# Ways out of PSUM in the first unit, and a filter block by sums, in a two-layer H3 and GEGLU kernel

## The chip, the cores and the metric

The kernel runs on one core of one Trainium2 chip, as one launch. The metric is the device time of one execution in microseconds (us); the median of a few runs is given, and one more execution was taken with the hardware profiler. The granted TensorE clock was 1.00 throughout.

## The reference, cut to what matters

Two layers over 2048 tokens of width D = 576, with the same weights twice:

```python
def A(q, k, v, shift_k, ssm_k, ssm_D):          # H3 mixer
    kv = causal_shift_conv(k, shift_k) * v       # 4 taps
    y = irfft(rfft(pad(kv)) * rfft(pad(ssm_k)))  # causal convolution, length 2048, per channel
    return q * (y + kv * ssm_D)

def B(x, w_gate, w_up, w_down):                  # F = 4608
    return (gelu(x @ w_gate) * (x @ w_up)) @ w_down

x = A_q
for layer in range(2):
    x = x + A(layernorm(x), A_k, A_v, A_shift_k, A_ssm_k, A_ssm_D)
    x = x + B(layernorm(x), B_w_gate, B_w_up, B_w_down)
```

The inputs are bfloat16. `k`, `v` and the filter `ssm_k` are the same in both layers, so the mixer's `y` is made once per token and used twice.

## The kernel before, in words

**Units.** The tokens lie in four chunks of 512. A unit is one chunk of one layer's GEGLU; there are eight. They run in five passes, unit 0 alone, three passes of two units, and the last unit alone. Each unit is cut into three phases of 12 f-tiles of 128. A phase first makes gate and up for its 12 f-tiles and then adds the down product of these 12 to the residual. A gate/up tile is 18 matmuls (L1585: nine blocks of 64 contraction rows, gate and up side by side in the two row halves of TensorE) into one PSUM tile `gu`, of two banks, gate in one and up in the other. ScalarE takes gelu of the gate bank into `ga` (L1589), VectorE multiplies `ga` by the up bank into `hT` (L1590), which releases the PSUM tile. The pool `pr` has three such tiles. The down product (L1605) takes the four blocks j of 128 tokens one after another, each 24 matmuls over the 12 f-tiles, two halves of D to each; f-tile `fi` is read by matmuls 2 fi and 2 fi + 1 of a block. In unit 0, phase 0 comes in two token halves (`half_gu`, L1510 to L1514), 6 + 6 tiles of two f-tiles each, since the second half's input isn't there yet.

**Convolution.** It is done in blocks of 512 tokens: the transform of the filter block (H), that of kv (kc), their products summed over pairs of blocks (z), and an inverse (L389) whose result ScalarE copies out (`keep_y`, L395). Every transform is a few matmuls of 288 columns with constant matrices `W`. `quarter` makes a transform by four sums: four visits to TensorE of two matmuls each (L289), each copied out by ScalarE into an `eo` tile (L292), then sums and differences on VectorE (`apart` L252, `odd` L257, `even` L265). H of filter block 1 was made another way: row 2 in the startup (L214) and rows 0, 1 and 3 by full transforms and sums (`h1_rest`: L214, L223) during unit 0.

**What sets the order.** The program order of every engine is decided when the kernel is built. A planner keeps an estimated time per engine (`t.pe`, `t.act`, `t.dve`, with costs such as `C_HT` and `C_GU`). After every gate/up tile and every down step it calls `fill`, which places queued VectorE work of the convolution and of the norms up to a limit, then ScalarE's, then visits of the convolution to TensorE, and the loads and DMA transposes that have come due (`weights`, `run_loads`, `spreads`). Each engine then works strictly in this order. Weight loads (`wgu`, `wd`), the transposes of the filter (`turn`, L429) and those that make the next unit's `xnT` (`spread`, L1290) are issued by SyncE; `k`, `v`, spills and reloads of H and kc by GpSimd.

**Around the change.** During unit 0 the convolution of block 1 is finished: H1 and kc 1, z 1, then the inverse in four visits (132.0, 135.1, 138.3, 141.4 us), each into the single PSUM tile `cps`. Its y gives the second chunk's input, which is normalised and transposed into `xnT` of unit 1 (SyncE, 143.6 to 156.3 us). Unit 1 begins at 158.35 us.

Of the kernel before, what the change touches and what calls it, by code (L numbers as in the profile page):

```python
# [39 lines left out]
C_TT, C_ST, C_HT, C_GELU, C_EVA, C_EVD = 0.76, 0.82, 0.69, 0.6, 0.66, 0.76  # L40
# [44 lines left out]
class Conv:  # L85
# [9 lines left out]
    def __init__(self, spare, tc, ctx, pace, A_k, A_v, A_shift_k, A_ssm_k, A_ssm_D, ident, psp, cpsp, ypool):  # L95
# [31 lines left out]
        self.h1_at = {2: 0.0}  # L127
        self.z_at, self.then = {}, []
        self.load_at, self.tight, self.turning = -9.0, lambda: False, lambda: False
        self.nps = 0  # L130
        self.ps_free = self.spare_free = self.last = 0.0
        self.window = -1.0
        self.pr_free = [0.0] * N_SM
        self.neo, self.eo_free = 0, [0.0] * N_EO
# [108 lines left out]
    def quarter(self, src, out, h, ready, seen, done):  # L243
# [3 lines left out]
        A, slots = {}, {}  # L247
# [7 lines left out]
        def even():  # L255
            for kt, op in ((0, add), (2, sub)):
                tt(out=out()[kt][:, :, cols], in0=A[2][:], in1=A[3][:], op=op)  # L257
            when = t.on_dve(2 * C_R4)
            self.eo_free[slots[2]] = self.eo_free[slots[3]] = when
            done(0, h, when + LAG)  # L260

        def odd():
            for kt, ops in ((1, (add, sub)), (3, (sub, add))):
                for s in range(2):
                    tt(out=out()[kt][:, s, cols], in0=A[0][:, s, :], in1=A[1][:, 1 - s, :], op=ops[s])  # L265
            when = t.on_dve(4 * C_BF)
            self.eo_free[slots[0]] = self.eo_free[slots[1]] = when
            done(1, h, when + LAG)
# [3 lines left out]
        def when():  # L272
            at = [g[1] for g in going]
            if todo:
                at.append(self.slot_at())
            return max(ready(), self.eo_slot(), min(at))

        def one(n):
            def run():
# [11 lines left out]
                A[i], slots[i] = self.eo_tile("eo")  # L291
# [32 lines left out]
    def eo_tile(self, name):  # L324
        slot = self.neo % N_EO
        self.neo += 1
        self.eo_free[slot] = NEVER
        return self.eop.tile([P, 2, HW], F32, tag="eo", name=name), slot

# [112 lines left out]
    def filt(self, b):  # L442
# [23 lines left out]
        for h in range(2):  # L466
            self.Pq.extend(self.quarter(lambda: own["t"], out, h, lambda: max(own.get("at", NEVER), self.z_at[b - 1]()), seen, done))
            self.Pq.extend(self.then)
            self.then = []

    def step(self, m, kv=None, loaded=False):
# [60 lines left out]
        for kt, a in pairs:  # L532
            self.L.append((lambda kt=kt, a=a: max(self.hr_free[self.nhr % N_HR] if (m, a) != (1, 0) else 0.0,
# [155 lines left out]
        for h in range(2):  # L689
            if h == 1 and m == 1:  # L690
                self.Pq.extend(self.rest[:4])
            self.Pq.extend(self.quarter(lambda: self.vt_[m], out4, h, get(("kv", h)), seen4, done4))
        if m == 1:
            self.Pq.extend(self.rest[4:])
# [14 lines left out]
        zt = lambda mt: get(("z", mt)) if quad else zs  # L709
        out = [(lambda g=zt(mt): max(g(), self.y_used.get(m - 2, NEVER) if m > 1 else 0.0), cost, inv(mt), m) for mt in range(RT)]  # L710
        if m == 2:
            self.then = out
        else:
# [62 lines left out]
    def h1_rest(self):  # L776
        nc, t = self.nc, self.t

        own = {}

        def even(s):
            def run():
                own.update(self.pair_tile(), free=NEVER, eo=self.spare())
                self.fwd_sum(own["ps"], self.hT1, 1, s, 0)
                nc.scalar.copy(out=self.halves(own["eo"][:]), in_=own["ps"][:, :, 0:HW])
                self.last = own["at"] = t.on_act(C_EVA, t.pe + 0.49 + LAG) + LAG
            return run

        def odd(s):
            def run():  # L790
                it = dict(own)
                self.fwd_sum(it["ps"], self.hT1, 1, s, 1)
                nc.scalar.copy(out=self.halves(self.H1[:, 1, s, :]), in_=it["ps"][:, :, 0:HW])
                self.last = done = t.on_act(C_EVA, t.pe + 0.49 + LAG) + LAG

                def fin():
                    self.differ(self.H1[:, 3, s, :], it["eo"], it["ps"])
                    when = own["free"] = t.on_dve(C_R4, t.pe) + LAG
                    self.pair_done(it, max(done, when))
                    if s == 1:  # L800
                        for k in (1, 3):
                            self.h1_at[k] = when
                            self.spill(self.Hd[1][k], self.H1[:, k, :, :], when)
                self.U.append((t.pe + 0.49 + LAG, C_R4, fin))
            return run

        def full(kt, s):
            def run():
                self.fwd_full(self.hT1, kt, s, self.H1[:, kt, :, :])
                self.ps_free = t.on_act(C_EVA, t.pe + 0.98 + LAG)  # L810
                if s == 1:
                    self.h1_at[kt] = self.ps_free + LAG
                    self.spill(self.Hd[1][kt], self.H1[:, kt, :, :], self.ps_free + LAG)
            return run
        tasks = [((lambda: max(own.get("free", 0.0), self.slot_at()), 0.49, even(s), None, "pair"),
                  (lambda: own["at"], 0.49, odd(s), None, "pair")) for s in range(2)]
        first = [(lambda: 0.0, 0.98, full(0, s)) for s in range(2)]
        self.rest = [first[0], tasks[0][0], first[1], tasks[0][1], *tasks[1]]

    def begin(self, head, tables):  # L820
# [4 lines left out]
        with ExitStack() as es:  # L825
# [9 lines left out]
            full = tmp.tile([P, 256], BF16, name="full")  # L835
# [8 lines left out]
            wx = [tmp.tile([P, RT, DW], BF16, name=f"wx{i}") for i in range(2)]  # L844

# [5 lines left out]
            nc.vector.memset(full[:], 1.0)  # L851
# [19 lines left out]
            def busy(n):  # L871
                for _ in range(n):
                    nc.tensor.matmul(idle[:, 0, 0:256], lhsT=full[:, 0:P], rhs=full[:], start=True, stop=True)  # L873
# [188 lines left out]
            h_part(1, 2, 0, None, small())  # L1062
            rest = h_part(1, 2, 1, None, new(), True)
# [4 lines left out]
            rest()  # L1068
            self.spill(self.Hd[1][2], self.H1[:, 2, :, :])
# [20 lines left out]
def ssm_geglu_kernel(ctx, tc, A_q, A_k, A_v, A_shift_k, A_ssm_k, A_ssm_D, B_x, B_w_gate, B_w_up,  # L1090
# [83 lines left out]
    def sum_task(c, j, v):  # L1174
        def run():
            v["s"] = small.tile([P, 1], F32, tag="s", name="s")
            junk = work.tile([P, D], BF16, tag="ga", name="junk")
# [11 lines left out]
    def square_task(get_x, v):  # L1189
        def run():  # L1190
            v["ss"] = small.tile([P, 1], F32, tag="ss", name="ss")
            junk = work.tile([P, D], BF16, tag="ga", name="junk")
# [57 lines left out]
    def prep(ui, j):  # L1250
# [3 lines left out]
        def norm(ready):  # L1254
# [4 lines left out]
            xn_made.append((ui, j, xn, t.on_act(C_NA, max(ready, t.pe - 1.0)) + 0.3))  # L1259

        def norm_v(j):
            def run():
# [5 lines left out]
                xn_made.append((ui, j, xn, t.dve + C_NV + 0.3))  # L1268
# [33 lines left out]
    def run_vq(limit):  # L1302
# [11 lines left out]
        if r > max(t.pe + 0.2, t.dve):  # L1314
# [39 lines left out]

    def fill(limit, tensor, conv_first):
        weights()
        conv.run_loads()
        spreads()
        while True:
# [10 lines left out]
        if tensor and (hurry() or t.pe > conv.last + (CHAINED if chained() else 0.0)):  # L1370
            for _ in range(3):
                if not conv.run_p():
                    break

    with tc.manual_schedule():
# [97 lines left out]
        def first_half(hT):  # L1473
# [7 lines left out]
            for n in range(FP // 2):  # L1481
                half_gu(hT, n, 0)
                t.pe += C_GU
                if n == 0:
# [7 lines left out]
                elif n < 4:  # L1492
                    j = 2 * n - 3
                    turn0(j)
                    copy0(j, nc.scalar.copy)
                if n == 2:
                    t.dve = t.act = t.pe + 1.6
                elif n > 2:
                    t.on_dve(C_HT, t.on_act(C_GELU, t.pe + 0.15) + 0.15)
# [3 lines left out]
        def half_gu(hT, n, half):  # L1503
            pair = psp.tile([P, 2, 512], F32, tag="pr", name="gu")
            xnT, tok = xnT_of[0], slice(half * 2 * P, (half + 1) * 2 * P)
            for e in range(2):
                w, gi = wgu[(2 * n + e) // FG], (2 * n + e) % FG
                for k in range(NKC):
                    for s, r0 in ((0, 0), (1, HK)):
                        nc.tensor.matmul(pair[:, s, e * 256:(e + 1) * 256], lhsT=w[r0:r0 + HK, k, gi * P:(gi + 1) * P],  # L1510
                                         rhs=xnT[r0:r0 + HK, blk_of[k], tok], start=(k == 0), stop=(k == NKC - 1))
            ga = work.tile([P, CH], F32, tag="ga", name="ga")
# [7 lines left out]
        for m in range(2, NCH):  # L1520
# [6 lines left out]
        at_start = {(0, 2): [("es", 1), ("prep", 1)], (1, 0): [("x", 2)], (2, 1): [("es", 2)],  # L1527
# [10 lines left out]
        conv.tight, conv.turning = chained, turns_near  # L1538
        visits = []
# [3 lines left out]
        for wb, ph, ui, first, final in visits:  # L1543
# [25 lines left out]
            if wb == 0:  # L1569
                first_half(hT)  # L1570
                for n in range(FP // 2):
                    half_gu(hT, n, 1)
                    t.pe = max(t.pe, free.popleft()) + C_GU
                    free.append(t.on_dve(C_HT, t.on_act(C_GELU, t.pe + 0.15) + 0.15) + 0.1)
# [3 lines left out]
            for fi in range(FP if wb else 0):  # L1578
# [9 lines left out]
                ga = work.tile([P, CH], F32, tag="ga", name="ga")  # L1588
                nc.scalar.activation(out=ga[:], in_=pair[:, 0, :], func=ACT.Gelu_apprx_tanh)  # L1589
                nc.vector.tensor_tensor(out=hT[:, fi, :], in0=ga[:], in1=pair[:, 1, :], op=ALU.mult)  # L1590
                free.append(t.on_dve(C_HT, t.on_act(C_GELU, t.pe + 0.15) + 0.15) + 0.1)
                if gi == FG - 1 and final:
                    when_due(t.pe + (FP - FG) * C_GU + 12.0, load_wgu, n + 3)
                fill(t.pe + C_GU + (HURRY if hurry() else LEAD), now(), conv.left > 0)
            conv.window = t.pe + RT * FP * C_DN - SPARE if wb < NWB - 1 else -1.0
# [100 lines left out]
```

## Time and profile before

| | us |
|---|---|
| Median of 3 runs | 915.8 (915.63 to 916.01) |
| Profiled execution | 916.32 |
| Its span | 914.3 |
| TensorE busy | 907.3 |
| VectorE, ScalarE, GpSimd busy | 577.3, 321.8, 160.6 |
| Start of gate/up in unit 0 | 39.47 |
| Down phases of unit 0 begin | 66.25, 106.43, 146.48 |

Lines of the timeline have: start, busy time, engine, line, operation, output<-input, shape, number of instructions in the row, and in brackets the idle time before it with what ended it. A row may hold several instructions, and their starts overlap with the end of the one ahead, so a step is read from start to start. Lines of the windows have the busy time and the number of instructions of each engine, then granted clock, DMA share and GB/s. Lines of DMA issues end with the median time from issue to landing. PE is TensorE, DVE VectorE, ACT ScalarE, POOL GpSimd, SP SyncE.

### The profile page before, as it was taken

How to read it: one execution, taken by the hardware profiler on the slowest of the kernel's cores; microseconds unless marked ns; L12 is line 12 of the kernel's file. 1: busy time of each engine (PE TensorE's matmuls, PEld its weight loads, DVE VectorE, ACT ScalarE, POOL GpSimd, SP SyncE). 2: the span in 40 equal slices, each digit the busy share in tenths (PEclk: the TensorE clock that was granted, in tenths of full speed). 3: DMA queues.
4: the chain of work that ended last, by engine and by line, in shares of the span. 5: the costliest groups of instructions: out<-in, count | busy, mean ns of one | idle time of the engine just before them, and what ended most of it. 6: DMA issues, size and time to landing. Idle time of an engine off the chain costs nothing.

```text
span 914.3 us, 19277 instructions
## 1 busy us (share of the span) xinstructions
PE 907.3 (99%) x8198; PEld 528.2 (58%) x8198; DVE 577.3 (63%) x982; ACT 321.8 (35%) x602; POOL 160.6 (18%) x334
## 2 busy tenths in 40 slices
PE   8999999999999999999999999999999999999998
PEld 6786556465565564654655655646646546556555
DVE  7988977479889885685698897443333335333332
ACT  6843255533214235452224124551121224321211
POOL 3512124320115032240013202220000003100000
PEclk9999999999999999999999999999999999999999
DMA  9999986939528619675734902950720821967620
GB/s 254 324 258 256 196 181 129 274 126 197 170 79 193 190 14 155 170 182 129 179 95 103 252 24 60 179 127 17 140 79 1 156 78 27 173 166 176 137 64 27
DMA packets 128954, 131.14 MB, mean 143 GB/s; under 512 B 43618, under 2 KB 120675, under 8 KB 128868
## 3 DMA queue, kind: packets, MB, share of 16 engines
q1 hardware_dynamic: 119232, 93.47, 48.3%
q0 software_dynamic: 9632, 36.43, 12.1%
q8 instruction: 64, 1.05, 0.5%
q14 instruction: 22, 0.18, 0.1%
q10 hardware_dynamic: 4, 0.01, 0.0%
HBM read 108.35 MB, written 11.80 MB: 131 GB/s over the span
## 4 chain that ended last, share of the span: by engine, by line
PE 98%; DVE 1%; ACT 1%; issue 0%; DVEq 0%; ACTq 0%
PE gu L1585 59%; PE dn L1605 31%; PE gu L1510 3%; PE ps L214 1%; PE cps L389 1%; PE cps L289 1%; DVE wx L936 0%; PE ps L389 0%; PE ps L289 0%; PE cps L214 0%; PE cps L873 0%; DVE wx L939 0%; ACT junk L1193 0%; PE xps L1403 0%; DVE v L930 0%; PE ps L950 0%
## 5 line engine op out<-in xcount | busy, mean ns | idle before, releaser
L1585 PE MATMUL gu<-xnT,wgu 64*128 64x512 bf16 x4968 | 540.8, 376 | 0.0
L1585 PEld LDWEIGHTS <-wgu 64*128 64x128 bf16 x4968 | 239.5, 94 | 294.4 <-issue 5.9
L1589 ACT ACTIVATE ga<-gu 128x512 f32<-128x512 f32 x276 | 164.6, 597 | 481.0 <-PE gu L1585 472.4
L1590 DVE TENSOR_TENSOR hT<-ga,gu 128x512 bf16<-128x512 f32 x276 | 189.5, 686 | 213.3 <-ACT ga L1589 211.1
L1605 PE MATMUL dn<-wd,hT 128*128 128x288 bf16 x2304 | 292.1, 286 | 0.0
L1605 PEld LDWEIGHTS <-hT 128*128 128x128 bf16 x2304 | 223.6, 98 | 65.4 <-issue 9.3
L1641 DVE TENSOR_TENSOR x_c<-x_c,dn 128x576 f32<-128x576 f32 x64 | 48.1, 752 | 57.3 <-PE dn L1605 57.3
L1185 POOL TENSOR_SCALAR nm<-s 128x1 f32<-128x1 f32 x60 | 22.0, 366 | 268.2 <-DVE x_c L1636 203.2
L1193 ACT ACTIVATE junk<-x_c,nm 128x576 bf16<-128x576 f32 x48 | 36.9, 769 | 30.1 <-POOL nm L1185 28.5
L1201 POOL TENSOR_TENSOR rstd<-ve,neghalf_t 128x1 f32<-128x1 f32 x62 | 41.8, 675 | 5.2
L529 POOL DMA_DIRECT2D hr<-Hd x32 | 17.5, 548 | 116.4 <-DVE prod L348 110.9
L1200 POOL TENSOR_SCALAR ve<-ss 128x1 f32<-128x1 f32 x62 | 25.2, 406 | 54.9 <-ACT junk L1193 54.7
L1257 ACT ACTIVATE xn<-x_c,nb,rstd 128x576 bf16<-128x576 f32 (+1 forms) x50 | 29.8, 644 | 6.9 <-POOL nb L1205 6.7
L1627 DVE TENSOR_TENSOR ob<-x_c,dn 128x576 bf16<-128x576 f32 x15 | 11.3, 754 | 23.1 <-PE dn L1605 20.8
L1510 PE MATMUL gu<-xnT,wgu 64*128 64x256 bf16 x432 | 24.6, 269 | 0.0
L292 ACT COPY eo<-cps 128x576 f32<-128x576 f32 x26 | 16.6, 637 | 19.3 <-PE cps L289 16.0
L349 DVE TENSOR_TENSOR prod<-prod 128x576 bf16<-128x576 bf16 x48 | 22.0, 458 | 1.7
L1510 PEld LDWEIGHTS <-wgu 64*128 64x128 bf16 x432 | 20.8, 94 | 3.4 <-issue 0.7
L404 POOL DMA_DIRECT2D out_dram<-ob x12 | 6.7, 558 | 81.7 <-DVE ob L1627 61.2
L252 DVE SCALAR_TENSOR_TENSOR eo<-eo 128x576 f32<-128x576 f32 x20 | 14.9, 753 | 6.6 <-ACT eo L292 6.6
L1235 DVE SCALAR_TENSOR_TENSOR x_c<-g_t,rstd,x_c 128x576 f32<-128x576 f32 x16 | 13.0, 814 | 9.3 <-POOL rstd L1201 9.3
L587 DVE TENSOR_TENSOR zs<-sum,prod 128x576 f32<-128x576 bf16 x24 | 18.1, 754 | 0.3
(168 smaller groups left out, 557.8 us busy)
## 6 DMA issues: line engine op xcount, KB each, us to landing
wgu<-in_B_w_gate_dram SPq DMA_DIRECT2D x45, 576.0 KB, 5.8
wd<-in_B_w_down_dram SPq DMA_DIRECT2D x30, 864.0 KB, 6.9
wgu<-in_B_w_up_dram SPq DMA_DIRECT2D x45, 512.0 KB, 8.0
hr<-Hd POOLq DMA_DIRECT2D x32, 288.0 KB, 4.7
kr<-Kd POOLq DMA_DIRECT2D x24, 288.0 KB, 4.7
Kd<-kc POOLq DMA_DIRECT2D x12, 288.0 KB, 5.1
k<-in_A_k_dram POOLq DMA_DIRECT2D x3, 1008.0 KB, 11.5
wgu<-in_B_w_up_dram SPq DMA_DIRECT2D x45, 64.0 KB, 7.6
```

What stands on the lines that cost most here:

```text
L349: nc.vector.tensor_tensor(out=dst, in0=pr[:, 0, :], in1=pr[:, 1, :], op=ALU.subtract if part == 0 else ALU.add)
L1185: nc.gpsimd.tensor_scalar(out=v["nm"][:], in0=v["s"][:], scalar1=-1.0 / D, scalar2=None, op0=ALU.mult)
L1193: nc.scalar.activation(out=junk[:], in_=get_x(), func=ACT.Square, bias=v["nm"][:, 0:1], accum_out=v["ss"][:])
L1200: nc.gpsimd.tensor_scalar(out=ve[:], in0=v["ss"][:], scalar1=1.0 / D, scalar2=EPS, op0=ALU.mult, op1=ALU.add)
L1201: nc.gpsimd.tensor_tensor(out=v["rstd"][:], in0=ve[:], in1=neghalf_t[:, 0:1], op=ALU.pow)
L1257: nc.scalar.activation(out=xn[:, lo:hi], in_=x_c[c][:, j, 0:hi - lo], func=ACT.Identity, scale=v["rstd"][:, 0:1], bias=v["nb"][:, 0:1])
L1510: nc.tensor.matmul(pair[:, s, e * 256:(e + 1) * 256], lhsT=w[r0:r0 + HK, k, gi * P:(gi + 1) * P], rhs=xnT[r0:r0 + HK, blk_of[k], tok], sta ...
L1585: nc.tensor.matmul(pair[:, s, :], lhsT=w[r0:r0 + HK, k, gi * P:(gi + 1) * P], rhs=xnT[r0:r0 + HK, b, :], start=(k == 0), stop=(k == NKC - 1))
L1589: nc.scalar.activation(out=ga[:], in_=pair[:, 0, :], func=ACT.Gelu_apprx_tanh)
L1590: nc.vector.tensor_tensor(out=hT[:, fi, :], in0=ga[:], in1=pair[:, 1, :], op=ALU.mult)
L1605: nc.tensor.matmul(part[h][:, h, 0:HW], lhsT=hT[:, fi, at * P:(at + 1) * P], rhs=wd[2 * wb + fi // WT][:, fi % WT, h * HW:(h + 1) * HW], s ...
L1641: nc.vector.tensor_tensor(out=xh, in0=xh, in1=acc[:, :, 0:HW], op=ALU.add)
```

## The change

- **H of filter block 1** is made wholly by `quarter`, in eight visits of two matmuls. As its `eo` tiles are needed elsewhere, the sums lie in tiles lent from the reload buffers `hr` and one spare tile. The row made in the startup goes there too. Visits lie in the first half tiles and the first down phase.
- **Unit 0's gates and ups** leave PSUM by ScalarE alone in 13 pairs of tiles (4 in phase 0, 6 in the second phase, 3 in the third): gelu to bfloat16 `ga2`, and a copy of up, rounded to bfloat16, into `hT`. VectorE then multiplies two tiles in one instruction from SBUF into `hT`. `fill` places that multiply at its start once the planner takes the pair for ready; a pair that is left when the loop over f-tiles ends is placed behind the last `fill`.
- **Block 1's inverse** comes in two visits of two, the second of each in a tile borrowed from `pr`.
- **The filter's turns.** `turn(2)` comes inside unit 0's first down phase, `turn(3)` in the second; block 2's first quarters move from the second unit's first down phase to the down phase ahead of unit 1. The load of `k` for block 2 waits until the transposes into unit 1's `xnT` have been issued in the plan (`clear`). Planner constants for the norms of unit 1 move, `junk` takes another buffer during unit 0, and `full` shares the memory of `wx`.

```diff
@@ quarter
-                A[i], slots[i] = self.eo_tile("eo")
+                A[i], free[i] = self.lent_tile() if lent else self.sum_tile()
@@ the steps of block m
-            self.L.append((lambda: max(self.kv_at.get(m - 1, NEVER), self.td_at.get(self.NB - 1, NEVER)), lk))
+            self.L.append((lambda: max(self.kv_at.get(m - 1, NEVER), self.td_at.get(self.NB - 1, NEVER), self.clear()), lk))
...
+            if (m, n) == (1, 2):
+                self.turn(2)
...
+        def inv_two(mts):
+            def run():
+                ...
+                two = [(mt, pool.tile([P, 2, 512], F32, tag=tag, name="ps"))
+                       for mt, pool, tag in zip(mts, (self.cpsp, self.psp), ("cps", "pr"))]
+                for n, (mt, ps) in enumerate(two):
+                    self.inverse(m, mt, self.terms(mt, z), ps)
+                    self.keep_y(m, mt, ps)
+                    ...
+        elif m == 1:
+            self.Pq.extend((zs, 2 * cost, inv_two(mts), m) for mts in ((0, 1), (2, 3)))
@@ h1_rest: the full transforms and sums go
+        out = lambda: {kt: self.H1[:, kt, :, :] for kt in range(RT)}
+        self.rest = [q for h in range(2) for q in self.quarter(lambda: self.hT1, out, h, lambda: 0.0, lambda h: None, done, True)]
@@ startup
-            h_part(1, 2, 0, None, small())
-            rest = h_part(1, 2, 1, None, new(), True)
...
-            rest()
-            self.spill(self.Hd[1][2], self.H1[:, 2, :, :])
@@ fill
+        while made and made[0][0] <= max(t.pe + 0.2, t.dve):
+            run_made()
@@ gates and ups
+        def hidden(dst, pair, e, count):
+            if e == 0:
+                while len(made) > 1:
+                    run_made()
+                two["ga"] = work.tile([P, 2, CH], BF16, tag="ga", name="ga2")
+            ga = two["ga"]
+            nc.scalar.activation(out=ga[:, e, :], in_=pair[:, 0, :], func=ACT.Gelu_apprx_tanh)
+            nc.scalar.copy(out=dst[:, e * count:(e + 1) * count, :], in_=pair[:, 1, :].rearrange("p (f q) -> p f q", f=count))
+            when = t.on_act(2 * C_GELU, t.pe + 0.15)
+            if e == 1:
+                made.append((when + 0.15, lambda: nc.vector.tensor_tensor(
+                    out=dst, in0=ga[:].rearrange("p e (f q) -> p (e f) q", f=count), in1=dst, op=ALU.mult)))
+            return when + 0.1
@@ the loop over f-tiles
+                if ui == 0 and (fi % 2 and rounded or fi % 2 == 0 and conv.left > 0):
+                    rounded = True
+                    free.append(hidden(hT[:, fi - fi % 2:fi - fi % 2 + 2, :], pair, fi % 2, 1))
+                else:
+                    rounded = False
                     ga = work.tile([P, CH], F32, tag="ga", name="ga")
                     ...
                 fill(t.pe + C_GU + (HURRY if hurry() else LEAD), now(), conv.left > 0)
+            conv.borrowed = None
+            while made:
+                run_made()
```

More of the change, by code (lines that the diff above doesn't have):

```diff
@@ L241, in fwd_eo, with quarter @@
         return eo, slot
-    def quarter(self, src, out, h, ready, seen, done):
+    def quarter(self, src, out, h, ready, seen, done, lent=False):
         nc, t = self.nc, self.t
         cols = slice(h * HW, (h + 1) * HW)
-        A, slots = {}, {}
+        A, free = {}, {}
         add, sub = ALU.add, ALU.subtract
@@ L328, in eo_tile, with sum_tile, lent_tile, free @@
         return self.eop.tile([P, 2, HW], F32, tag="eo", name=name), slot
+    def sum_tile(self):
+        tile, slot = self.eo_tile("eo")
+        return tile, lambda when: self.eo_free.__setitem__(slot, when)
+    def lent_tile(self):
+        at, self.nlent = self.nlent % 4, self.nlent + 1
+        if at == 3:
+            self.lent_free, tile = NEVER, self.spare()
+            def free(when):
+                self.lent_free = when
+        else:
+            slot, tile = self.nhr % N_HR, self.hrp.tile([P, 2, HW], F32, tag="hr", name="eo")
+            self.hr_free[slot] = NEVER
+            self.nhr += 1
+            def free(when):
+                self.hr_free[slot] = when
+        return (self.halves(tile[:]) if at == 3 else tile), free
+    def lent_slot(self):
+        return (self.lent_free if self.nlent % 4 == 3 else self.hr_free[self.nhr % N_HR]) - 0.7
     def eo_slot(self):
@@ L466, in filt @@
         for h in range(2):
-            self.Pq.extend(self.quarter(lambda: own["t"], out, h, lambda: max(own.get("at", NEVER), self.z_at[b - 1]()), seen, done))
+            self.Pq.extend(self.quarter(lambda: own["t"], out, h, lambda: max(own.get("at", NEVER), self.z_at[b - 1](), self.clear()), seen, done))
             self.Pq.extend(self.then)
@@ L531, in load @@
             return run
-        for kt, a in pairs:
-            self.L.append((lambda kt=kt, a=a: max(self.hr_free[self.nhr % N_HR] if (m, a) != (1, 0) else 0.0,
+        for n, (kt, a) in enumerate(pairs):
+            if (m, n) == (1, 2):
+                self.turn(2)
+            self.L.append((lambda kt=kt, a=a: max(self.hr_free[self.nhr % N_HR] if (m, a) != (1, 0) else 0.0, NEVER if (m, a) == (1, 1) and self.nlent < 8 else 0.0,
                                            self.kr_free[self.nkr % 3] if a < m else 0.0,
@@ L776, in h1_rest @@
     def h1_rest(self):
[L777 to L816, printed above, removed]
@@ L817, in h1_rest, with done @@
-        first = [(lambda: 0.0, 0.98, full(0, s)) for s in range(2)]
-        self.rest = [first[0], tasks[0][0], first[1], tasks[0][1], *tasks[1]]
+        def done(kt, h, when):
+            if h == 1:
+                for k in (kt, kt + 2):
+                    self.h1_at[k] = when
+                    self.spill(self.Hd[1][k], self.H1[:, k, :, :], when)
+        out = lambda: {kt: self.H1[:, kt, :, :] for kt in range(RT)}
+        self.rest = [q for h in range(2) for q in self.quarter(lambda: self.hT1, out, h, lambda: 0.0, lambda h: None, done, True)]
@@ L872, in busy @@
                 for _ in range(n):
-                    nc.tensor.matmul(idle[:, 0, 0:256], lhsT=full[:, 0:P], rhs=full[:], start=True, stop=True)
+                    nc.tensor.matmul(idle[:, 0, 0:256], lhsT=full[:, 0:P], rhs=full, start=True, stop=True)
             busy(8)
@@ L1176, in run @@
             v["s"] = small.tile([P, 1], F32, tag="s", name="s")
-            junk = work.tile([P, D], BF16, tag="ga", name="junk")
+            junk = junk_tile()
             nc.scalar.activation(out=junk[:], in_=x_b[c][:, j, :], func=ACT.Copy, accum_out=v["s"][:])
@@ L1191, in run @@
             v["ss"] = small.tile([P, 1], F32, tag="ss", name="ss")
-            junk = work.tile([P, D], BF16, tag="ga", name="junk")
+            junk = junk_tile()
             nc.scalar.activation(out=junk[:], in_=get_x(), func=ACT.Square, bias=v["nm"][:, 0:1],
@@ L1353, in chained, with run_made, junk_tile @@
         return bool(aq or nq) or need is not None and not (need[0] == "y2" and need[1:3] not in conv.y_at)
+    made = deque()
+    def run_made():
+        ready, run = made.popleft()
+        run()
+        t.on_dve(C_H2, ready)
+    def junk_tile():
+        return work.tile([P, D], BF16, tag="ob" if unit0 else "ga", name="junk")
+    unit0 = [0]
     def fill(limit, tensor, conv_first):
@@ L1373, in fill @@
                     break
+        if unit0 and conv.borrowed:
+            while run_vq(limit, t.pe + C_GU):
+                pass
     with tc.manual_schedule():
@@ L1511, in half_gu @@
                                          rhs=xnT[r0:r0 + HK, blk_of[k], tok], start=(k == 0), stop=(k == NKC - 1))
+            if not old:
+                return lambda: hidden(hT[:, 4 * (n // 2):4 * (n // 2) + 4, tok], pair, n % 2, 2)
             ga = work.tile([P, CH], F32, tag="ga", name="ga")
@@ L1587, in ssm_geglu_kernel @@
                 t.pe = max(t.pe, free.popleft()) + C_GU
[L1588 to L1591, printed above, removed]
+                if ui == 0 and (fi % 2 and rounded or fi % 2 == 0 and conv.left > 0):
+                    rounded = True
+                    free.append(hidden(hT[:, fi - fi % 2:fi - fi % 2 + 2, :], pair, fi % 2, 1))
+                else:
+                    rounded = False
+                    ga = work.tile([P, CH], F32, tag="ga", name="ga")
+                    nc.scalar.activation(out=ga[:], in_=pair[:, 0, :], func=ACT.Gelu_apprx_tanh)
+                    nc.vector.tensor_tensor(out=hT[:, fi, :], in0=ga[:], in1=pair[:, 1, :], op=ALU.mult)
+                    free.append(t.on_dve(C_HT, t.on_act(C_GELU, t.pe + 0.15) + 0.15) + 0.1)
+                if conv.borrowed:
+                    free.popleft()
+                    free.append(conv.borrowed)
+                    conv.borrowed = None
                 if gi == FG - 1 and final:
@@ L1594, in ssm_geglu_kernel @@
                 fill(t.pe + C_GU + (HURRY if hurry() else LEAD), now(), conv.left > 0)
+            conv.borrowed = None
+            while made:
+                run_made()
+            if ui == 0 and end:
+                unit0.clear()
             conv.window = t.pe + RT * FP * C_DN - SPARE if wb < NWB - 1 else -1.0
```

64 lines of the change are left out of this document (40 added, 24 removed).

## The prediction

> **What bounds the kernel now.** I read the page's busy times and chain first, then the windows, then single stretches of the timeline. The page:
>
> ```profile
> PE 907.3 (99%) x8198; PEld 528.2 (58%) x8198; DVE 577.3 (63%) x982; ACT 321.8 (35%) x602; POOL 160.6 (18%) x334
> ...
> PE 98%; DVE 1%; ACT 1%; issue 0%; DVEq 0%; ACTq 0%
> ...
> L1590 DVE TENSOR_TENSOR hT<-ga,gu 128x512 bf16<-128x512 f32 x276 | 189.5, 686 | 213.3 <-ACT ga L1589 211.1
> ```
>
> PE is the bound: of its 7.0 us without work 3.8 lie in the first 40 us and 3.2 behind the last matmul. In between it never stops, as the windows show for the stretch that holds nearly all of the change:
>
> ```profile
> 40.00:147.00 107.00, 107.00 (x1153) 68.13 (x1150) 91.88 (x159) 44.95 (x87) 23.01 (x44) 1.00 0.94 218
> ```
>
> (PE busy 107.00 of 107.00; DVE 91.88; ACT 44.95; granted clock 1.00; DMA share 0.94.) So after 40 us only two things count: PE work that is added or removed, and any place where PE must now wait. A shorter DVE or ACT queue is worth nothing by itself. The span is 914.3, the execution 916.32, 0.5 above the median 915.8; I sum differences and set them on the median.
>
> **Matmuls removed: -1.96.** H1 of filter block 1 took 16 matmuls of L214 in the startup and 16 of L214 plus 16 of L223 between 67.7 and 79.7; four sums need 8 visits of two, 16 in all. In the profile eight L214 matmuls hold PE for .98 (67.72 to 68.70), .1225 each. Behind 40 us that is 32 before and 16 after: 16 x .1225 = 1.96. The startup's 16 are in the next step.
>
> **Startup: -0.3.** The other 16 matmuls (1.96) and two ACT copies of H (.62 each) also go. Yet DVE works without a gap from 25 to 37.2 and its list there is unchanged. What is freed is a PE wait for ACT ahead of the inverse of Y3:
>
> ```profile
> 38.39 1.14 PE L389 MATMUL ps<-yb,W 128*128 128x288 bf16 x8 [0.67 <-ACT xnT L1410]
> ```
>
> So gate and up start some .7 earlier, at about 38.7 instead of 39.47. The fourth half tile, however, needs the PSUM that DVE's second hT multiply releases, and DVE is late there:
>
> ```profile
> 45.38 0.69 DVE L1514 TENSOR_TENSOR hT<-ga,gu 128x512 bf16<-128x512 f32 x1
> 46.12 1.14 PE L1510 MATMUL gu<-xnT,wgu 64*128 64x256 bf16 x17
> ```
>
> 45.38 + .69 = 46.07, and PE goes on at 46.12. That time stays; PE waits there instead. All that is kept is one quarter visit (two matmuls, .25 to .35) which the change puts ahead of this point: -0.3, with bounds 0 and -0.75 (had DVE been early).
>
> **Two visits instead of four: -0.42.** Block 1's inverse interrupts gate and up:
>
> ```profile
> 132.00 1.15 PE L389 MATMUL cps<-yb,W 128*128 128x288 bf16 x8
> 133.08 2.12 PE L1585 MATMUL gu<-xnT,wgu 64*128 64x512 bf16 x18
> 135.13 1.15 PE L389 MATMUL cps<-yb,W 128*128 128x288 bf16 x8
> ```
>
> One round is 135.13 - 132.00 = 3.13. Eight matmuls in a row cost .98, a gate/up tile of 18 elsewhere 1.95 (23.4 for 12): .20 is lost at each change of shape and back. The whole phase, 118.36 to 146.55, gives .21. Two fewer: -.42. The first visit comes no earlier, as z is complete on DVE at 130.33 and the visit at 132.00 was within 1.7 of that.
>
> **A late quarter: +0.2.** One visit of a later filter now falls inside a gate/up phase; a quarter there took .35 instead of .25 and the tile behind it .08 longer, +.19. The other quarters only change their place inside down phases, where two 288-wide shapes follow each other at .1225.
>
> **Pairs in unit 0: nothing for the arithmetic.** Thirteen pairs: ACT does gelu and a copy per tile, DVE one bf16 product of 1024 per pair. No row has that product. The 1152-wide one takes .75 and the 576-wide .46, so by the line between them .69 (bounds .46 and 1.22, the 1024-wide product from PSUM at 13.81). DVE drops 26 x .69 = 17.9 and gains 13 x .69 = 9.0; the four sums add about 9 (L252 .75, L265 .37, L257 .7). ACT gains 26 copies of about .57 (a 576-wide copy from PSUM, L292, takes .64), 15 us in a stretch where it is busy 45 of 107. PSUM comes free about 1.2 behind the last matmul of a tile (gelu starts .1 after it, .50 to the copy, .6), while three buffers leave 3.9: cover 2.7, enough for any single ACT row (.96 the longest). With two such rows queued ahead it would still hold.
>
> The Trainium skill ("VectorE: DVE Perf Modes", Rules for kernel authors) says of products on matmul output to take the slow rate, or to copy out of PSUM first if many operations follow; here one follows. The rows side with the rule on engine time (9 us less DVE for 15 us more ACT), and by it the pairs would best be left out: the sum would lose the stall of the next paragraph and be 913.5.
>
> **A new wait: +1.5.** In the phase from 83 to 118 (second third of unit 0) the last pair is multiplied only after the filter work that the planner places behind the last tile. Before, the last multiply stood early enough:
>
> ```profile
> 103.89 1.42 DVE L363 TENSOR_TENSOR yb<-zs 128x576 bf16<-128x576 f32 x2
> 105.22 0.69 DVE L1590 TENSOR_TENSOR hT<-ga,gu 128x512 bf16<-128x512 f32 x1
> 105.83 0.75 DVE L346 TENSOR_TENSOR prod<-kr,H 128x1152 bf16<-128x1152 bf16 x1
> 106.61 0.46 DVE L349 TENSOR_TENSOR sum<-prod 128x576 bf16<-128x576 bf16 x1
> 106.99 0.75 DVE L348 TENSOR_TENSOR prod<-kr,H 128x1152 bf16<-128x1152 bf16 x1
> 107.78 0.46 DVE L349 TENSOR_TENSOR sum<-prod 128x576 bf16<-128x576 bf16 x1
> 108.15 0.68 DVE L1590 TENSOR_TENSOR hT<-ga,gu 128x512 bf16<-128x512 f32 x1
> ```
>
> The down phase starts at 106.43 and reaches f-tile 11 with matmul 22, at 106.43 + 22 x .1225 = 109.13; hT was there at 108.83. Now count from the start T of that down phase in the changed kernel. Tile 9 ends two tiles earlier, T - 3.90; gelu, copy: its pair can be multiplied at T - 2.66. The changed order then puts on DVE: that product .60, two yb sums .78, a product .79 and its half .49, zs .79, two yb 1.33, a product .78 and half .38 (spacings of L370, L346, L349, L587, L363), 5.9 in all; the last pair starts at T + 3.25 and is done at T + 3.9. PE needs f-tile 10 with matmul 20, at T + 2.45. The weight load (.1) included, PE waits 1.5. Bounds: 0 if the filter work shortens by that much, 2.2 if the 1024-wide product costs its upper bound. The other two phases end with no such work ahead.
>
> **k against the last transposes: +0.2.** The load of k for block 2 (1008 KB, POOL) moves into the end of unit 0, between the transposes that make unit 1's xnT. Two windows of before, first without and then with such a load:
>
> ```profile
> xnT<-xn SPq DMA_TRANSPOSE x2, 2.5
> ```
>
> ```profile
> k<-in_A_k_dram POOLq DMA_DIRECT2D x1, 1008.0 KB, 6.1
> xnT<-xn SPq DMA_TRANSPOSE x2, 4.6
> ```
>
> Before, the last transpose was issued at 155.01, landed at 157.5 and unit 1 began at 158.35, 3.34 after the issue. Two quarter visits now stretch the down phase behind it by .98, so 4.3. Alone the transpose needs 2.5, beside k 4.6: late by 0.3, taken as +0.2; bounds 0 and 2.1 (6.4, as between 172 and 174).
>
> **Sum.** -1.96 - 0.30 - 0.42 + 0.19 + 1.5 + 0.2 = -0.8; 915.8 - 0.8 = **915.0**. The turns of the filter move earlier on SP, ahead of weight loads; those land over 15 us before their use, which covers the 7 to 8.4 of a turn. With that cover gone, PE would wait for a weight load.
>
> **Rivals.** A: the wait of 1.5 does not arise, because DVE reaches the last pair in time. For: DVE has been relieved of 9 us, and PE need only be as slow as the chain. Against: the chain begins at a copy, not at a backlog, so relief elsewhere does not shorten it. Then -2.3 to -2.5: 913.4. B: the change's pairs are no faster than the products from PSUM (1.22 for two): DVE gets 16 instead of 9 us, the last pair is .55 later, 915.6; same verdict as the forecast. C, slower: k's megabyte holds unit 1's transposes. Next to two loads of wd and one of x_b they took far longer:
>
> ```profile
> xnT<-xn SPq DMA_TRANSPOSE x1, 10.9
> ```
>
> At 8.5 to 10.9 instead of 4.6 the last lands 4.2 to 6.6 after PE wants it: 919 to 921. It turns slower than before once the transpose takes over 5.3, and measurably so from about 7.1. For: wgu is issued 1.3 behind the last transpose too, and DMA is at a share near 1. Against: k alone gave 4.6. The Trainium skill ("DMA: Bandwidth & Descriptors", Issuing engines are not separate DMA queues) has all queues share the same 16 engines, so POOL's queue would be no shelter; the 2.5 and 4.6 agree.
>
> **How the numbers follow.** About 0.2% (1.8 us: below 914.0, above 917.6) is what a measurement of this kernel can tell from no change. The forecast with B and the smaller half of C's prices: 0.48. A: 0.36; it takes in stalls below .5 and a startup that keeps more of its .75. C and whatever other wait costs over 2.6: 0.16. Range 912.9 (A with the whole startup) to 917.8; the likeliest case alone holds 914.2 to 916.2.
>
> **What would show it.** PE rows: 8166 matmuls. A PE idle of about 1.5 some 2.5 us into the down phase near 106, released by DVE at the pair's multiply; half of the rivals falls with that one line. The inverse as two rows of x16 some 1.95 + .2 apart from gate/up. The fourth half tile still near 46.1, with a PE idle ahead of it. At unit 1's first matmul an idle of 0 to .5, released by DMA; over 3 would mean C. Wrong would be: a PE idle elsewhere, above all for ACT's release of PSUM or at filter block 2's earlier visits.

## The result, and the profile after

The changed kernel takes 920.78 us (median of 5, 919.29 to 922.01) against 916.01 for the kernel before (5 runs): a ratio of 1.0051, 95% interval 1.0036 to 1.0066. It is slower, by 4.8 us; the forecast was 915.0 in a range of 912.9 to 917.8. The profiled execution took 919.29 with a span of 917.5, so 3.2 above the span of before. The other 1.5 up to the median is not in this execution; the first experiment finds it.

From the page after, the lines that answer to those of before:

```profile
PE 902.6 (98%) x8166; PEld 526.5 (57%) x8166; DVE 577.1 (63%) x983; ACT 334.3 (36%) x628; POOL 160.1 (17%) x334
...
PE 92%; DVE 3%; DMA 2%; ACT 1%; SPq 1%; POOL 1%; issue 0%; DVEq 0%; POOLq 0%; ACTq 0%
```

PE has 32 matmuls less and works 4.7 us less, yet the span is longer: its time without work went from 7.0 to 14.9. The chain that ended last says through whom: DVE, DMA, SP's queue and POOL now stand in it. The longest waits of PE name the places (total, times, longest):

```profile
PE gu L1635 <- DMA xnT<-xn: 4.1, 2, 3.2
PE xps L1429 <- DVE xn L1413: 2.7, 1, 2.7
PE dn L1669 <- DVE hT L1546: 1.4, 1, 1.4
```

Starts of phases, read from the timelines of both kernels, make the ledger:

| Start of | before | after | difference | what changed it |
|---|---|---|---|---|
| gate/up, unit 0 | 39.47 | 38.31 | -1.16 | startup |
| its first down phase | 66.25 | 65.79 | -0.46 | fourth half tile waits for DVE; one quarter visit more ahead of it |
| second gate/up | 83.01 | 80.36 | -2.65 | H1's matmuls |
| third gate/up | 118.29 | 117.18 | -1.11 | wait for the pair |
| third down phase | 146.48 | 144.94 | -1.54 | two visits, not four |
| unit 1 | 158.35 | 161.04 | +2.69 | wait for xnT, and .98 of quarter visits that come earlier |
| next gate/up | 195.59 | 197.47 | +1.88 | those visits missing here |
| a down phase, pass 4 | 616.92 | 620.05 | +3.13 | second wait for xnT; late quarter |

From there to the end it stays at +3.1. A wait is counted from the modelled end of the matmul ahead and the ledger from start to start, so each wait weighs 0.17 more in the ledger than in brackets (20 matmuls of the down phase take 2.45 from start to start, their row below 2.62).

The lines behind these steps follow. First the startup and the fourth half tile, which goes on as soon as DVE's second multiply (44.93, for 0.68) is done:

```profile
35.07 0.68 PE L1429 MATMUL xps<-ident,xn 128*128 128x128 bf16 x9 [2.69 <-DVE xn L1413]
```

```profile
45.67 2.14 PE L1557 MATMUL gu<-xnT,wgu 64*128 64x256 bf16 x36
```

The inverse in two visits of 16, a round of 4.11 (136.94 - 132.83) with two inverses in it:

```profile
132.83 2.13 PE L416 MATMUL ps<-yb,W 128*128 128x288 bf16 x16
134.89 2.12 PE L1635 MATMUL gu<-xnT,wgu 64*128 64x512 bf16 x18
```

The last pair of the second phase on DVE, and the down phase that waits for it:

```profile
101.10 0.69 DVE L1546 TENSOR_TENSOR hT<-ga,hT 128x1024 bf16<-128x1024 bf16 x1 [0.56 <-ACT hT L1543]
101.71 0.82 DVE L397 TENSOR_TENSOR yb<-yb 128x576 bf16<-128x576 bf16 x2
102.45 0.75 DVE L375 TENSOR_TENSOR prod<-kc,hr 128x1152 bf16<-128x1152 bf16 x1
103.23 0.46 DVE L376 TENSOR_TENSOR prod<-prod 128x576 bf16<-128x576 bf16 x1
103.72 0.76 DVE L616 TENSOR_TENSOR zs<-sum,prod 128x576 f32<-128x576 bf16 x1
104.52 1.43 DVE L390 TENSOR_TENSOR yb<-zs 128x576 bf16<-128x576 f32 x2
105.86 0.75 DVE L373 TENSOR_TENSOR prod<-kr,H 128x1152 bf16<-128x1152 bf16 x1
106.65 0.46 DVE L376 TENSOR_TENSOR sum<-prod 128x576 bf16<-128x576 bf16 x1
107.03 0.68 DVE L1546 TENSOR_TENSOR hT<-ga,hT 128x1024 bf16<-128x1024 bf16 x1
```

```profile
103.77 2.62 PE L1669 MATMUL dn<-wd,hT 128*128 128x288 bf16 x20
107.76 4.46 PE L1669 MATMUL dn<-wd,hT 128*128 128x288 bf16 x35 [1.37 <-DVE hT L1546]
```

And k's load with the transposes issued beside it and just behind it, from two windows (150.5 to 152, 153.5 to 155), then PE:

```profile
k<-in_A_k_dram POOLq DMA_DIRECT2D x1, 1008.0 KB, 8.5
xnT<-xn SPq DMA_TRANSPOSE x2, 6.9
```

```profile
xnT<-xn SPq DMA_TRANSPOSE x2, 7.1
```

```profile
161.04 9.18 PE L1635 MATMUL gu<-xnT,wgu 64*128 64x512 bf16 x82 [3.19 <-DMA xnT<-xn]
```

### The profile page after: what moved, and what is told of

It is laid out like the page before. It is cut to its first block, busy times and chain, and to the rows that moved or that the text cites. A ratio compares the mean times of both kernels' runs of the same rounds, so it can differ in the third digit from the quotient of the medians.

```text
span 917.5 us, 19235 instructions
## 1 busy us (share of the span) xinstructions
PE 902.6 (98%) x8166; PEld 526.5 (57%) x8166; DVE 577.1 (63%) x983; ACT 334.3 (36%) x628; POOL 160.1 (17%) x334
## 4 chain that ended last, share of the span: by engine, by line
PE 92%; DVE 3%; DMA 2%; ACT 1%; SPq 1%; POOL 1%; issue 0%; DVEq 0%; POOLq 0%; ACTq 0%
PE gu L1635 58%; PE dn L1669 28%; PE gu L1557 2%; DMA xnT<-xn 2%; PE ps L217 1%; PE cps L292 1%; PE ps L416 1%; PE cps L416 1%; SPq L1298 0%; PE ps L292 0%; DVE wx L948 0%; DVE x_c L1460 0%; DVE x_c L1457 0%; POOL rstd L1209 0%; PE cps L885 0%
## 5 line engine op out<-in xcount | busy, mean ns | idle before, releaser
L1644 ACT ACTIVATE ga<-gu 128x512 f32<-128x512 f32 x258 | 154.0, 597 | 467.8 <-PE gu L1635 460.8
L1645 DVE TENSOR_TENSOR hT<-ga,gu 128x512 bf16<-128x512 f32 x258 | 177.0, 686 | 205.0 <-ACT ga L1644 203.5
L1542 ACT ACTIVATE ga<-gu 128x512 bf16<-128x512 f32 x26 | 15.5, 597 | 33.4 <-PE gu L1635 26.4
L295 ACT COPY eo<-cps 128x576 f32<-128x576 f32 x29 | 18.6, 640 | 20.4 <-PE cps L292 16.8
```

## The experiments

The times are medians of 5 runs (e1, e4, e6), 11 (e2, e3, e5) or 6 (e7, e8); the kernel before stood at 916.04 to 916.07 beside them. "W" and the other letters are theories, told in the expectations. "Half clock" is a granted TensorE clock of 0.50.

### e1: the changed kernel again

No edit.

> The changed kernel once more, on the chip of the other three. Theory W (the loss is three waits of PE: 3.2 us for the transposes into unit 1's xnT, 1.4 for the last pair of the second phase, 0.9 for transposes of a later unit): 919 to 922, and a profile with the same three waits, the first of them different from run to run. Rival R (the loss is spread, the waits are an accident of one execution): the wait before unit 1 is under 1 us and the time still near 920.8.

Measured: 920.8 (919.08 to 922.09). The three waits are there (3.4 and 0.7 for xnT, 1.4 for the pair), the first nearly the same as before, so it does not make the spread. What does is the granted clock. The same four microseconds in the profiled execution of the result and in this one (third from last column):

```profile
36.00:37.00 1.00, 1.00 (x12) 0.64 (x11) 0.93 (x4) 0.67 (x2) 0.00 (x0) 1.00 1.02 400
37.00:38.00 1.00, 1.00 (x14) 0.85 (x13) 0.68 (x2) 0.58 (x2) 0.00 (x0) 1.00 1.10 420
38.00:39.00 1.00, 1.00 (x18) 0.69 (x17) 0.34 (x1) 0.98 (x3) 0.00 (x0) 1.00 1.00 327
39.00:40.00 1.00, 1.00 (x24) 0.89 (x20) 1.00 (x3) 0.99 (x3) 0.00 (x0) 1.00 0.97 354
```

```profile
36.00:37.00 1.00, 1.00 (x8) 0.65 (x7) 0.93 (x5) 0.88 (x2) 0.00 (x0) 0.73 1.00 393
37.00:38.00 1.00, 1.00 (x11) 0.94 (x10) 0.55 (x3) 0.00 (x0) 0.00 (x0) 0.50 1.08 421
38.00:39.00 1.00, 1.00 (x8) 0.65 (x6) 0.34 (x1) 0.73 (x2) 0.00 (x0) 0.50 1.04 342
39.00:40.00 1.00, 1.00 (x5) 0.44 (x3) 0.49 (x1) 0.98 (x2) 0.00 (x0) 0.57 1.00 349
```

Behind PE's gap of 2.7 in the startup the clock falls to half for 3.4 us, and again from 162.7 to 166.2, behind the wait for xnT. This span is 920.3, 2.8 above 917.5. The second gate/up begins 1.2 later than in the result (81.55 against 80.36); 0.2 of that stands already at 22.5 us, ahead of the stretch, so the first stretch costs 1.0. The second costs 1.6: the first 216 matmuls of unit 1 take 25.23 instead of 23.64. The wait itself is 0.2 longer. The five runs of the result fit: 919.3 and 919.5 with a mean clock of 1.000, 920.8 with 0.998, 921.8 and 922.0 with 0.996. So the missing 1.5 is one such stretch in the middle run; which of the two places it was in isn't on record.

### e2 and e3: k earlier, k later

```diff
# e2
-            self.L.append((lambda: max(self.kv_at.get(m - 1, NEVER), self.td_at.get(self.NB - 1, NEVER), self.clear()), lk))
+            self.L.append((lambda: max(self.kv_at.get(m - 1, NEVER), self.td_at.get(self.NB - 1, NEVER)), lk))
# e3, the same line
+            self.L.append((lambda: max(self.kv_at.get(m - 1, NEVER), self.td_at.get(self.NB - 1, NEVER), self.clear(), self.begun()), lk))
...  (begun is set when the visit of unit 1 starts)
```

> The load of k for block 2 no longer waits until unit 1's transposes are planned; GpSimd issues it about 11 us sooner, ahead of the first of them. Theory W: the last four transposes land in 2.5 to 3 us again instead of 7, PE's wait before unit 1 (3.2) goes wholly, and the time falls by 3 to 4.5, to about 917. Rival D (DMA is full in that stretch with or without k, share near 1): the transposes still take over 5 us and the time falls by less than 1.

> The load of k for block 2 is held until unit 1 has begun, some 8 us later than in the changed kernel. Theory W: as with the early load, wait before unit 1 gone, about 917; the transposes into the next unit's xnT (needed 35 us later) take the contention and nobody waits. Rival D: the wait stays near 3, the time near 920.8.

Measured: 916.32 (915.43 to 917.31) and 916.92 (915.59 to 917.36), 4.5 and 3.9 below the changed kernel. GpSimd issued k at 141.59 and 161.52 instead of 151.66. The transposes of the window 153 to 155 landed in 4.0 and 4.3 (W had 2.5 to 3; e8 tells why), PE did not wait before unit 1 in either, and there is no half clock near 162. The rival that DMA is full with or without k is out. Executions with a mean clock of 1.000 stand at 915.7 in both, against 919.1 to 919.5 of the changed kernel (result and e1), so the wait, the pipeline it empties and a slightly shorter wait at the later unit are worth 3.6; the rest of the 4.5 and 3.9 is the half clock behind it. The half clock in the startup stays: both profiles show it (35.8 to 39.2 and 34.8 to 38.2), 15 of the 22 executions have a mean clock of 0.998, and these are 1.1 (e2) and 1.3 (e3) slower than the others.

### e4: the pair first

```diff
                 if gi == FG - 1 and final:
                     when_due(t.pe + (FP - FG) * C_GU + 12.0, load_wgu, n + 3)
+                while fi == FP - 1 and made:
+                    run_made()
                 fill(t.pe + C_GU + (HURRY if hurry() else LEAD), now(), conv.left > 0)
```

> At the last f-tile of a phase of unit 0 the multiply of the pair is placed ahead of the filter work instead of behind it; nothing else changes. Theory W: PE's wait of 1.4 in the down phase near 105 goes, time 1.4 lower than the changed kernel, about 919.4. Rival Q (VectorE is in arrears there, so the wait only moves): the multiply is still late by over 0.7, or the inverse of block 1 waits instead, and the time falls by less than 0.7.

Measured: 919.45 (918.67 to 920.68), 1.35 below the changed kernel; both medians are of executions with one stretch of half clock. DVE now waits for ScalarE's copy and multiplies at once, and the down phase runs through (66 matmuls in one row):

```profile
105.23 0.69 DVE L1546 TENSOR_TENSOR hT<-ga,hT 128x1024 bf16<-128x1024 bf16 x1 [0.50 <-ACT hT L1543]
```

```profile
104.02 8.26 PE L1671 MATMUL dn<-wd,hT 128*128 128x288 bf16 x66
```

The wait did not move elsewhere: those for xnT are 3.1 and 0.7.

### e5: the gap in the startup filled

```diff
-            head.turn(0, 8)
+            head.turn(0, 42)
```

> The changed kernel with 34 more idle transposes (128x128, about 0.07 us each) where TensorE waits 2.7 us in the startup; k and the pair as in the changed kernel. Theory G (the half clock that some executions show from 36 to 39.6 us follows from that gap; it costs up to 1.4 us): no granted clock under 1.00 before 40 us in the profile, the wait of 2.7 down to about 0.3, the median 0.5 to 1 lower (about 920), and what spread is left comes from the other gap, ahead of unit 1. Rival N (the half clock is chance and has nothing to do with the gap): median and spread as in the changed kernel, 920.8 and 919 to 922.

Measured: 916.62 (915.91 to 917.03), 4.2 below the changed kernel. The gap is 0.8, there is no half clock before 40 us, the mean clock is 1.000 in all 11 executions, and the spread is 1.1. So far G holds. But its 0.5 to 1 is far too small. The waits for xnT had changed as well: 1.1 instead of 3.2 before unit 1 (and no half clock behind it), none at the later unit. Filling a gap at 33 us had moved something at 155 us. The DMA rows show a candidate. In the changed kernel from 151 to 152, then 155 to 156:

```profile
q1 hardware_dynamic: 519, 0.12, 64.9%
q8 instruction: 1, 0.02, 7.8%
```

```profile
q0 software_dynamic: 46, 0.37, 99.8%
```

and in e5 from 155 to 156:

```profile
q0 software_dynamic: 43, 0.35, 98.4%
q1 hardware_dynamic: 43, 0.01, 4.8%
```

Queue q8 carries instructions: 64 loads of 16 KB in all. TensorE's rows count 16,332 matmuls and weight loads, so one load per about 256 of them; that the loads are TensorE's is inferred from this. In the changed kernel one of them (151.9 us) falls among the transposes (q1). From 155 to 156 k's packets (q0) go alone, and from 157.4 to 159.4 only one or two packets of k start in each 0.4 us before the rest of the transposes moves. In e5 the 34 extra transposes with their weight loads, 68 instructions, bring that load 4.2 us forward, to 147.7, and k and the transposes share packet by packet. At the later unit it is alike: in the changed kernel the load is at 594.5, 1.1 ahead of the gate and up that then stop for xnT (595.59), and at 584.5 in the kernel before and 584.7 in e5, where nobody waits. That wait, 0.5 to 0.9, is in all five profiles with 8166 matmuls (result, e1 to e4).

### e6: the three repairs together

Edits of e2, e4 and e5.

> Early k, the pair's multiply first, and the filled gap together. Theory W with G: what is left of the change is its ledger without waits, -2.0 for 16 matmuls, -0.4 for two visits, -0.7 at the start, +0.2 for a late quarter and +0.5 to 0.9 for the transposes of a later unit: 913.6 to 914.5, faster than before by 0.2%, and the spread as narrow as before's 0.8. Rival S (waits that are removed come back elsewhere): over 915.5.

Measured: **913.22** (912.96 to 913.35), ratio 0.9968 (0.9956 to 0.9980): faster than the kernel before by 2.85, 0.4 more than was expected at best. Of PE's waits only those of the startup are left, the clock is 1.000, and the spread is 0.4. The ledger against before ends at -2.67: -0.5 for the startup, -1.94 for the matmuls, -0.43 for the two visits, +0.2 for the late quarter.

### e7: the same without pairs

```diff
# the edits of e6, and in hidden:
...
-            nc.scalar.activation(out=ga[:, e, :], in_=pair[:, 0, :], func=ACT.Gelu_apprx_tanh)
-            nc.scalar.copy(out=dst[:, e * count:(e + 1) * count, :], in_=pair[:, 1, :].rearrange("p (f q) -> p f q", f=count))
...
+            ga = work.tile([P, CH], F32, tag="ga", name="ga")
+            nc.scalar.activation(out=ga[:], in_=pair[:, 0, :], func=ACT.Gelu_apprx_tanh)
+            nc.vector.tensor_tensor(out=dst[:, e * count:(e + 1) * count, :], in0=ga[:].rearrange("p (f q) -> p f q", f=count),
+                                    in1=pair[:, 1, :].rearrange("p (f q) -> p f q", f=count), op=ALU.mult)
```

> As the run with all three repairs, but unit 0's gates and ups leave PSUM as before the change (gelu by ScalarE in float32, one VectorE multiply per tile from PSUM), no pairs; the planner places the rest anew. Theory P (the pairs earn nothing by themselves, TensorE being the bound, as the prediction had it): within 0.5 of the run with all three. Rival V (VectorE has to take 9 us of sums for the new H1 and 9 us of multiplies with it, so block 1's inverse and with it unit 1's xnT come late): the second inverse visit slips past 150 us, PE waits 8 to 15 us ahead of unit 1, and the time is 921 to 930.

Measured: 938.8 (934.12 to 942.83). V, and well above its 921 to 930:

```profile
PE gu L1629 <- DMA xnT<-xn: 18.4, 1, 18.4
```

```profile
155.58 2.12 PE L416 MATMUL ps<-yb,W 128*128 128x288 bf16 x16 [1.45 <-ACT y L422]
```

The two visits of the inverse stand at 152.01 and 155.58, behind all of unit 0's work (in e6 at 131.49 and 135.60), and unit 1 begins at 176.12 instead of 156.45. In this execution the clock is at half from 160.5 to 181.0 on top. The planner also placed other work anew, so 25.6 us is the price of taking the pairs out of this program, not that of the multiplies alone.

### e8: the instruction loads moved, the gap left

```diff
             pair = psp.tile([P, 2, 512], F32, tag="pr", name="gu")
+            if (n, half) == (5, 0):
+                for _ in range(34):
+                    nc.tensor.matmul(pair[:, 0, 0:P], lhsT=ident[:], rhs=ident[:], start=True, stop=True)
```

> The changed kernel with the same 34 small matmuls as in the filled run, but put where they fill nothing: in a row inside the first half tiles near 52 us, 2 us of extra TensorE work; the gap in the startup stays at 2.7 us. What they do is move every later load of TensorE's instructions (one per 256 instructions) some 4 us ahead of the work. Theory F (in the changed kernel such a load falls among unit 1's transposes and k, and holds one DMA engine back): the wait before unit 1 falls from 3.2 to about 1.1, that of the later unit (0.9) goes, and the time is 920.8 + 2.2 - 2.1 - 0.9 or a little less, near 919.5; half clock near 36 to 39 us stays possible. Rival B (filling the gap helped, the place of the instruction load is of no account): the wait before unit 1 stays at 3.1 to 3.4 and the time is about 923.

Measured: 919.2 (918.18 to 920.22), though it does 2.07 us more work. Without that work it would be 917.1, 3.7 below the changed kernel. By executions with a mean clock of 1.000 it is 918.8 - 2.07 = 916.7, as low as e5's 916.6, against 919.1 to 919.5; so e5's gain is some 2.7 from the loads, and the other 1.5 is half clock that no longer occurs. The wait before unit 1 is 1.9, between what F (1.1) and B (3.2) had; the one at the later unit is gone, and k's packets no longer end in a trickle. B is out: the gap was not touched. F has the later unit; before unit 1 it explains a good part, and what is left of the wait is k itself, as e2 and e3 show. That k's packets go alone isn't the load's doing: from 157 to 158 they still do here (50 of k, none of the transposes).

What a load does by itself can be read where k is far away. In the kernel before, transposes into unit 1's xnT land in 2.5 to 2.6, but the one issued at 148.0 in 4.2; a load starts at 150.0. In e2 and e3 those beside the load (153.0 and 154.2) took 4.0 and 4.3, in e5 and e8 (147.7 and 150.1) 4.0 and 4.5. So a load costs a transpose 1.5 to 2. The kernel before had one there too, with time to spare; what is new before unit 1 is k. Beside k without a load the transposes took 4.9 to 6.7 (e5, e8), with both 6.9 and 7.1.

## Why the prediction was wrong, point by point

- **Matmuls removed (-1.96), two visits (-0.42), late quarter (+0.2).** Right, in size and place. From the first down phase to the second gate/up the ledger gains 2.19, of which 0.25 is a quarter visit already done, so 1.94; the two visits gain 0.43; the quarter costs 0.2. (The phase read as 118.36 to 146.55 stands at 118.29 to 146.48 in the rows, of the same length.)
- **Startup (-0.3).** Right in kind: gate and up start earlier and the fourth half tile gives most of it back, as it hangs on DVE's second multiply. DVE was itself 0.45 earlier (its multiply at 44.93, not 45.38; the tile at 45.67, not 46.12), so with the quarter visit -0.7. Of this 0.25 is chance: DVE is that much early at 22.5 us already, where nine profiles differ by up to 0.5, and e6 without it has -0.5. (DVE's stretch from 25 to 37.2 has a gap of 0.27 at 27.5, in both kernels; nothing hangs on it.) What the step missed is that 2.7 us without matmuls can be followed by half clock, which costs 1.0 to 1.3 (e1 to e3).
- **Pairs: nothing for the arithmetic.** The 1024-wide product took 0.69, as drawn between two rows. That DVE's relief is worth nothing, and that leaving the pairs out would give 913.5, was wrong: I counted only DVE's rows beside PE, not when block 1's z and y must be ready. With nine more us of sums and no pairs, they are late (e7). The rule of the Trainium skill ("VectorE: DVE Perf Modes", Rules for kernel authors) is to copy out of PSUM first only ahead of many operations; here one follows, and the program without the copy was 25.6 slower, as what stands behind the multiplies in DVE's queue came late.
- **The new wait (+1.5).** Right, and for the reason given: the pair ahead is multiplied 2.67 before the down phase starts and the last one 3.26 behind it (2.66 and 3.25 in the prediction). PE waits 1.37, and with the wait removed the time falls by 1.35 (e4).
- **k against the last transposes (+0.2).** This step failed: it had the landing, and with it the wait, too small. It took 4.6 as the landing beside k, from one window of before in which the transpose was issued 1.2 ahead of k (177.54, k at 178.72); it was 6.9 to 7.1. The time left for it was shorter too: the last transpose was issued at 154.30, 3.5 before unit 1 could have begun (144.94 + 11.87 for the down phase + .98 = 157.8) and not 4.3, since SP took 2.05 instead of 1.3 to issue the one ahead. The wait was 3.2 instead of 0.2. That k causes it is shown by e2 and e3; a load of instructions makes some 1.3 of it (e8). Rival C named this place, its sign (an idle over 3) and its price by landing (5.3 to turn slower; at 7.1 it gives 1.8 slower). With all other waits over 2.6 it had 0.16, since I set the bound by the nearest row where the row of 10.9 was as near in kind.
- **What no case priced.** The wait at the later unit (0.9) and the half clock (1.5 in the median). Both come of removing work from PE. With 64 fewer instructions the loads fall elsewhere; the one in question moved from 584.5 to 594.5, and putting 68 back moves it away again (e5, e8). Why it moves by as much as 10 us is open, as 64 instructions are a quarter of a load. The half clock comes because the work had kept PE busy.

Sum for the profiled execution: -0.7 - 1.94 - 0.43 + 0.2 + 1.4 + 3.2 + 0.9 = +2.6, and 0.17 for each of the three waits: +3.1, the ledger's value. With the half clock of the median run, 1.5, it is 4.6 of the 4.8 measured. Without waits and half clock rival A's 913.4 was the sum, and e6 reaches 913.2.

## What to carry to other kernels

Where one engine is busy 99% of the time, ask of every change which transfer it puts beside a transfer that somebody waits for, and take the longest landing that the trace shows for that kind, not the nearest. Work that is taken off such an engine can cost in two ways: a gap where it stood, and a shift of the loads of its instructions against other transfers. Queue order at the end of a phase is worth a look by hand: one multiply placed behind other work, not its cost, made 1.4 us.

## What the runs showed of the hardware

- A gap of 2.7 us in PE's work came with half clock for 3.4 us in three of the six profiles that have it (e1, e2, e3), beginning 0.5 before to 1.2 behind its end, and with none in the other three. Behind the wait of 3.1 to 3.4 before unit 1 it came in two of three (e1 and e4, not in the result), behind that of 1.9 (e8) not. With the gap filled to 0.8 no execution of 11 had it. The Trainium skill ("TensorE: Matmul & The Clock Gate", Part 1) describes a free-running window of about 3.4 us whose idleness halves the clock. The length of 3.4 and the chance agree; that a gap shorter than the window was enough is measured here.
- Loads of instructions (16 KB, one per about 256 instructions of PE) share the DMA with other transfers. A transpose in flight when one came landed in 4.0 to 4.5 us instead of 2.5 in five profiles, with k nowhere near.
- Between k's packets and the transposes the Trainium skill ("DMA: Bandwidth & Descriptors", Queues, rings and completion order) has each engine take turns packet by packet. In e5 that is so, 43 to 43 in a microsecond; in the changed kernel it was 46 to none, and in e8 50 to none. Why is open.
